# A spectral mixing layer feeding a snake MLP on one core: two groups of a batch's last transform stage go behind the next batch's first stage, and three idle matmuls are added in the head

## The chip, the core and the metric

The kernel runs on one core of a Trainium2 chip. The engines that matter here are PE (TensorE: matmuls, with its weight loads shown as PEld), ACT (ScalarE), DVE (VectorE), POOL (GpSimd) and SP (SyncE); the last two mostly issue DMAs in this kernel. Each engine works through its own list of instructions in the order in which the program wrote them, and engines wait for one another through semaphores. The metric is the device time of one execution in microseconds (us).

## The reference, cut to what matters

```python
batch, seq, dim = (8, 3008, 256)          # d_ff = 2048
X = np.fft.rfft(x, axis=1)
Y = X * (filt_r + 1j * filt_i)[None, :, :]
y = np.fft.irfft(Y, n=seq, axis=1)        # 24064 rows of 256
h = y.reshape(24064, 256) @ w_in
s = np.sin(alpha * h)
g = h + s * s / (alpha + 1e-09)
return g @ w_out                          # float32
```

Each of the 8 sequences is filtered in the frequency domain, and the filtered rows go through a two-layer network whose activation is the snake function.

## The kernel before, in words

**Transforms.** The length 3008 is split into 47 x 64. A batch goes through four matmul stages, with an elementwise product in the middle: `first` (a transform over 47 points, PSUM tiles `pa`), `forward` (over 64 points, `pb`), the product with the filter on DVE, `inverse` (`pc`) and `last` (`pd`), which writes the time-domain rows, transposed, into the SBUF array `y`. Between `first` and `forward`, and between `inverse` and `last`, the data goes through DRAM to change its layout: `first` stores to `d1` (SP queue) and `load_t2` loads from it (POOL queue). Batch 0 takes a path of its own in the head, with transposes on DVE in place of the trips through DRAM, and its last stage is `last_0(n0, n, ...)`: the group of `n` rows of the split that begins at `n0`, in two halves, `cb` 0 and `cb` 1. Each half is `n` small matmuls of 94 columns into one PSUM bank, and then a cast into `y`, on ACT for half 0 and on DVE for half 1. A group covers the columns 94 n0 to 94 (n0 + n) - 1 of `y`.

**The network.** `y` of a pair of batches is cut into chunks of 512 columns (one of the twelve of a pair is 384 wide). `hidden(k, jb)` computes one of 16 blocks of the hidden layer for chunk k: two matmuls (`ph`, one for each half `cb` of `y`), a sine on ACT (`cos_all`), and on DVE an operation that makes the activation `v`. `project(k, u)` multiplies `v` by `w2` (`po`, eight matmuls in a call), and now and then ACT copies the result out (`o`), which is stored by DMA.

**The order.** The order of instructions is written out by hand. The main loop runs in steps; a chunk takes 8 steps, k runs from 0. Step s (with j = s mod 8) issues `hidden(k, 2j)` and `hidden(k, 2j+1)`, then a slot at s, then the `project` calls of chunk k-1, then a slot at s + 0.5. So chunk 2, columns 1024 to 1535, begins at step 16, and it reads `y` columns that the groups at 11 (columns 1034 to 1409) and at 15 (1410 to 1785) write. Everything of the transforms is put into one list, `pending`, with a due step, and `slot` takes from its front what is due; a PE item that is less than a step late is taken alone:

```python
while pending and pending[0][0] <= at:
    if pending[0][2]:
        if run and pending[0][0] > at - 1:
            break
        run += 1
```

Batch 1's sixteen `first` matmuls are due at `6.9 + 0.35 * i`, so the last ones at 11.1, 11.45, 11.8 and 12.15; its `load_t2` are due at 12.5, and its first `forward` at 18. A `last_0` group that is called with `spread=True` doesn't issue its matmuls at once: it puts them into the list `between`, and `one_between()` takes one after each `hidden` matmul and after each second `project` matmul.

**Buffers.** PSUM has the pool `fps` (2 banks: `pa`, `pb`, `pc`, `pd`), `hps` (4 banks: `ph`, and in the head also the idle `warm` tiles and others) and `ops` (2 banks: `po`). A matmul that takes a bank over waits until the cast of the bank's previous tile is done.

**Who casts.** `evac` decides between ACT and DVE. Its counter moves on at every call, also where the caller names the engine:

```python
flip[0] = (flip[0] + 1) % 3
if flip[0] if on_act is None else on_act:
```

The `first` matmuls let the counter decide, the `last_0` groups name the engine; so moving a group among the `first` matmuls also changes which engine casts some of these.

**The head.** `warm_pe(n)` issues `n` matmuls on a tile of zeros, into an `hps` bank that nobody reads. After batch 0's first stage come `spread_alpha(0)` (12 matmuls, `al_bc`), `inverse_table(0)` and `inverse_table(1)` (32 transposes, `pse`, that read the table `d_t`, which a DMA brings), `spread_alpha(1)`, one idle matmul and the first `forward_0` blocks (`pb`). The lines: `warm_pe` 443, `spread_alpha` 354, `inverse_table` 432, `last_0` 409, `first` 206, `forward` 243, `hidden` 610 (matmul), 614 (sine) and 615 (DVE), `project` 630, casts 185 (ACT) and 187 (DVE), `load_t2` 235, the loop over the groups 709 and 710.

Of the kernel before, what the change touches and what calls it, by code (L numbers as in the profile page):

```python
# [71 lines left out]
def kernel(  # L72
# [276 lines left out]
    def spread_alpha(i):  # L349

        ps = hps.tile([128, 4, 128], FP32, name=f"al_bc_{i}", tag="h")
        for a in range(4):
            for k, part in enumerate(parts):
                nc.tensor.matmul(out=ps[:, a, :], lhsT=one[:, 4 * i + a:4 * i + a + 1].to_broadcast([128, 128]),
                                 rhs=part, start=(k == 0), stop=(k == 2))
        nc.scalar.copy(out=alpha[:, i // 2, 512 * (i % 2):512 * (i % 2) + 512], in_=ps.rearrange("p a b -> p (a b)"))
# [69 lines left out]
    def inverse_table(g):  # L426

        gs = slice(8 * g, 8 * g + 8)
        ps = ops.tile([128, 8, 128], FP16, name=f"pse_{g}", tag="o")
        for i in range(8):  # L430
            for a in range(2):
                nc.tensor.transpose(out=ps[64 * a:64 * a + 64, i, :],
                                    in_=d_t[:, 8 * g + i, 64 - 64 * a:128 - 64 * a], identity=id16)
        nc.scalar.mul(e1_0[:, gs, :], ps, -0.125)
# [3 lines left out]
    def warm_pe(n):  # L438

        warmed.append(n)  # L440
        ps = hps.tile([128, 512], FP32, name=f"warm_{len(warmed)}", tag="h")
        for i in range(n):
            nc.tensor.matmul(out=ps, lhsT=idle[:, 0:128], rhs=idle[:, 0:512], start=True, stop=True)
# [18 lines left out]
    for i in range(16):  # L462
# [7 lines left out]
        if i < 15 and i % 4 == 3:  # L470
            warm_pe((1, 2, 2, 1)[i // 4])
    spread_alpha(0)
    [inverse_table(g) for g in range(2)]
    spread_alpha(1)
    warm_pe((2, 2, 2, 1)[3])
# [205 lines left out]
    def put(at, fn, *args, pe=False):  # L681
        pending.append((at, len(pending), pe, fn, args))
# [23 lines left out]
    for jb in range(12, 16):  # L706
        put(5 + 0.5 * (jb - 12), weights_out, jb, 1)

    for n0, n, at in ((6, 5, 1.5), (11, 4, 11), (15, 4, 13), (19, 4, 14.4), (23, 4, 15.6), (27, 5, 16.8)):
        put(at, last_0, n0, n, fps, "f", True)  # L710
    for b in range(1, B):
        s = s1 if b == 1 else Spectral(b)
# [89 lines left out]
```

## Time and profile before

| | |
|---|---|
| runs | 773.33, 773.35 and 774.28 us; median 773.35 us |
| the profiled execution, its own time | 774.35 us |
| its span, first to last instruction | 772.6 us |
| granted PE clock | 1.00 |
| PE busy | 763.0 us, 99% of the span |
| DVE, ACT, POOL busy | 655.4, 610.9, 373.1 us |
| HBM traffic | 133 GB/s over the span |

The profile page gives, for one execution, the busy time of each engine, the chain of work that ended last, and the costliest groups of instructions. The timeline gives rows of the form: start in us, duration in us, engine, line of the kernel, operation, output<-inputs, shapes, number of instructions merged into the row, and, where the engine was idle before it, the idle time and what ended it. A matmul's duration runs from its start to the arrival of its last result, while the next matmul may start earlier. So a short stall of PE hides under the durations and is not shown as idle; it is read from the distance between starts. In the steady part of this kernel a `first` matmul (`pa`) takes 0.22 us from start to start, a `ph` of 512 columns 0.216, a `po` 0.109 and a `pd` 0.04.

### The profile page before, as it was taken

The numbers are of one execution on the slowest core, as the hardware profiler recorded it, in microseconds if no ns is written. First come the engines' busy times: TensorE is split into PE (matmuls) and PEld (weight loads), VectorE is DVE, ScalarE is ACT, GpSimd is POOL, SyncE is SP. The second block draws the span as 40 slices with busy tenths as digits, with TensorE's granted clock in tenths as the row PEclk, the third lists the DMA queues.
The fourth block names the chain that finished last, engine by engine and source line by source line (L and its number), as shares of the span: only waits on it lengthen the run. The fifth ranks groups of instructions, "written<-read, shape, count | busy, mean of one in ns | idle before, by whom it ended". The sixth has DMA issues, their size and how long they took to land.

```text
span 772.6 us, 17227 instructions
## 1 busy us (share of the span) xinstructions
PE 763.0 (99%) x6038; PEld 517.1 (67%) x6038; DVE 655.4 (85%) x1171; ACT 610.9 (79%) x1205; POOL 373.1 (48%) x652
## 2 busy tenths in 40 slices
PE   8999999999999999999999999999999999999997
PEld 4757766666666667666666676766666766766666
DVE  7887998999988888988889888899888888777774
ACT  6898987898787878877878787888778787777763
POOL 7555455644636456545555646644554645520000
PEclk9999999999999999999999999999999999999999
DMA  9945678854854437544574536754254322511112
GB/s 225 292 108 167 139 172 257 205 131 112 219 145 125 114 92 207 140 114 118 118 197 114 137 94 156 196 144 121 72 145 109 90 69 56 147 35 33 40 36 61
DMA packets 81598, 101.49 MB, mean 131 GB/s; under 512 B 18900, under 2 KB 60880, under 8 KB 81511
## 3 DMA queue, kind: packets, MB, share of 16 engines
q0 software_dynamic: 27520, 47.29, 26.0%
q1 hardware_dynamic: 53426, 52.41, 25.5%
q8 instruction: 47, 0.77, 0.4%
q10 hardware_dynamic: 565, 0.70, 0.3%
q14 instruction: 40, 0.33, 0.1%
HBM read 56.15 MB, written 46.66 MB: 133 GB/s over the span
## 4 chain that ended last, share of the span: by engine, by line
PE 89%; DVE 5%; DMA 2%; ACT 2%; POOL 1%; issue 1%; SPq 0%; POOLq 0%; DVEq 0%
PE po L630 40%; PE ph L610 40%; DVE v L615 3%; PE pd L316 2%; PE pb L243 2%; PE pa L222 2%; DMA xs<-xf 1%; PE pc L293 1%; DMA e_t<-e_tbl 1%; ACT cos_all L614 1%; DVE t_a L479 1%; ACT t_h L185 1%; PE pa L206 0%; PE pd L409 0%; POOL filt_t L365 0%
## 5 line engine op out<-in xcount | busy, mean ns | idle before, releaser
L615 DVE SCALAR_TENSOR_TENSOR v<-cos_all,ph 128x512 f16<-128x512 f32 (+1 forms) x768 | 482.5, 671 | 94.8 <-ACT cos_all L614 90.8
L614 ACT ACTIVATE cos_all<-ph 128x512 f32<-128x512 f32 (+1 forms) x768 | 414.1, 600 | 99.4 <-PE ph L610 98.8
L675 POOL DMA_DIRECT2D out_dram<-o x530 | 291.7, 557 | 246.0 <-ACT o L639 219.5
L610 PE MATMUL ph<-y,w 128*128 128x512 f16 (+1 forms) x1536 | 389.3, 375 | 1.6 <-DVE v L615 1.3
L630 PE MATMUL po<-w,v 128*128 128x256 f16 x3008 | 389.5, 273 | 0.0
L630 PEld LDWEIGHTS <-v 128*128 128x128 f16 x3008 | 290.0, 98 | 84.2 <-issue 0.9
L610 PEld LDWEIGHTS <-w 128*128 128x128 f16 x1536 | 143.3, 98 | 114.1 <-issue 19.3
L639 ACT COPY o<-po 128x512 f32<-128x512 f32 (+1 forms) x95 | 56.0, 590 | 7.7 <-PE po L630 6.8
L185 ACT CAST y<-pd 128x376 f16<-128x376 f32 (+1 forms) x86 | 42.0, 490 | 13.1 <-PE pd L316 8.8
L246 ACT CAST xf<-pb 128x512 f16<-128x512 f32 x84 | 51.0, 608 | 0.9 <-PE pb L243 0.2
L160 POOL DMA_DIRECT2D x<-in_x_dram x48 | 25.6, 538 | 39.0 <-DVE v L615 29.9
L185 ACT CAST t_h<-pa 128x512 f16<-128x512 f32 (+1 forms) x60 | 32.8, 589 | 12.6 <-PE pa L222 11.3
L316 PEld LDWEIGHTS <-t_a 96*128 96x128 f16 x448 | 31.4, 97 | 12.7
L264 DVE TENSOR_TENSOR p<-p,xs 128x512 f16<-128x512 f16 x84 | 35.7, 425 | 2.9
L263 DVE TENSOR_TENSOR xs<-xs,filt_t 128x512 f16<-128x512 f16 x84 | 35.1, 418 | 3.5 <-DMA xs<-xf 3.5
L257 DVE TENSOR_TENSOR p<-xf,filt_t 128x512 f16<-128x512 f16 x84 | 35.0, 418 | 0.0
L185 ACT CAST gt<-pc 128x512 f16<-128x512 f32 x54 | 28.1, 595 | 8.4 <-PE pc L293 8.4
L187 DVE CAST t_h<-pa 128x512 f16<-128x512 f32 (+1 forms) x52 | 33.5, 682 | 0.2
L243 PE MATMUL pb<-t,d_t 128*128 128x256 f16 x168 | 32.1, 273 | 0.0
L316 PE MATMUL pd<-wh_t,t_a 96*128 96x94 f16 x384 | 31.8, 204 | 0.0
L235 POOL DMA_DIRECT2D t<-d x28 | 24.4, 874 | 10.7 <-DMA d<-t_h 10.0
L243 PEld LDWEIGHTS <-d_t 128*128 128x128 f16 x168 | 16.4, 98 | 14.3
(72 smaller groups left out, 276.5 us busy)
## 6 DMA issues: line engine op xcount, KB each, us to landing
t<-d POOLq DMA_DIRECT2D x28, 384.0 KB, 5.0
xs<-xf SPq DMA_DIRECT2D x168, 64.0 KB
t_a<-d SPq DMA_DIRECT2D x28, 384.0 KB
x<-in_x_dram POOLq DMA_DIRECT2D x50, 188.0 KB, 4.4
d<-t_h SPq DMA_DIRECT2D x48, 192.0 KB
d<-gt SPq DMA_DIRECT2D x36, 256.0 KB
out_dram<-o POOLq DMA_DIRECT2D x91, 64.0 KB, 2.1
out_dram<-o POOLq DMA_DIRECT2D x31, 80.0 KB, 3.3
```

The lines of the kernel that those rows point to most:

```text
L185: marks["act"] = nc.scalar.copy(out=dst, in_=src)
L243: nc.tensor.matmul(out=ps[:, i, :], lhsT=d_t[:, s, :], rhs=self.t2[s // 6][:, s % 6, :], start=True, stop=True)
L246: nc.scalar.copy(out=self.xf[u], in_=ps)
L263: nc.vector.tensor_tensor(out=xs, in0=xs, in1=f_t[1][:, 2 * u:2 * u + 2, :], op=ALU.mult)
L264: nc.vector.tensor_tensor(out=p, in0=p, in1=xs, op=ALU.add)
L316: nc.tensor.matmul(out=psv[:, i, :], rhs=wi_t if self.b < TILED else wh_t, start=True, stop=True, lhsT=t4_h[ch // 2][0:NK, n0 % 16 + i, cb ...
L610: nc.tensor.matmul(out=ps[:, 0:n], lhsT=w1[:, cb, jb * 128:jb * 128 + 128], rhs=y_cols[:, cb, c0:c0 + n], start=(cb == 0), stop=(cb == 1))
L614: nc.scalar.activation(out=cs[:, 0:n], in_=ps[:, 0:n], func=AFT.Sin, bias=float(np.pi / 2))
L615: marks["snake"] = nc.vector.scalar_tensor_tensor(out=v[k][:, jb, 0:n], in0=cs[:, 0:n], scalar=-1.0, in1=ps[:, 0:n], op0=ALU.add, op1=ALU. ...
L630: nc.tensor.matmul(out=pso[k][:, t % 2, :], lhsT=v[k][:, jb, 128 * t:128 * t + 128], rhs=w2[:, jb, :], start=(jb == 0), stop=(jb == 15))
L639: copy(out=o[:, i0:t % 2 + 1, :], in_=pso[k][:, i0:t % 2 + 1, :])
L675: queues[i % len(queues)].dma_start(out=bass.AP(tensor=out.tensor, offset=out.offset + t0 * C, ap=[*ap, [1, C]]), in_=o_blk[p0:p0 + rows, :])
```

## The change

```diff
@@ -470,6 +470,7 @@
         if i < 15 and i % 4 == 3:
             warm_pe((1, 2, 2, 1)[i // 4])
     spread_alpha(0)
+    warm_pe(3)
     [inverse_table(g) for g in range(2)]
     spread_alpha(1)
     warm_pe((2, 2, 2, 1)[3])
@@ -706,7 +707,7 @@
     for jb in range(12, 16):
         put(5 + 0.5 * (jb - 12), weights_out, jb, 1)
 
-    for n0, n, at in ((6, 5, 1.5), (11, 4, 11), (15, 4, 13), (19, 4, 14.4), (23, 4, 15.6), (27, 5, 16.8)):
+    for n0, n, at in ((6, 5, 1.5), (11, 4, 12.2), (15, 4, 13.2), (19, 4, 14.4), (23, 4, 15.6), (27, 5, 16.8)):
         put(at, last_0, n0, n, fps, "f", True)
     for b in range(1, B):
         s = s1 if b == 1 else Spectral(b)
```

Three idle matmuls of 512 columns go between `spread_alpha(0)` and the transposes of `inverse_table`, into one `hps` bank. The group at 11 goes from due step 11 to 12.2, behind batch 1's `first` matmuls 12 to 15; the group at 15 goes from 13 to 13.2. No other due step changes, and nothing else is added or removed.

## The prediction

> **What bounds the kernel.** I read the page's first part and the chain, then the busy time in stretches, then the timelines of the two places that the change touches.
>
> ```profile
> PE 763.0 (99%) x6038; PEld 517.1 (67%) x6038; DVE 655.4 (85%) x1171; ACT 610.9 (79%) x1205; POOL 373.1 (48%) x652
> PE 89%; DVE 5%; DMA 2%; ACT 2%; POOL 1%; issue 1%; SPq 0%; POOLq 0%; DVEq 0%
> ```
>
> PE is the bound and carries 89% of the chain. The stretches (start:end, length, then busy PE, PEld, DVE, ACT, POOL, clock, DMA) say whether a delay of PE can be made up later:
>
> ```profile
> 55.00:64.00 9.00, 8.79 (x71) 6.76 (x70) 5.52 (x10) 7.92 (x17) 3.67 (x7) 1.00 0.44 130
> 64.00:70.00 6.00, 6.00 (x58) 5.02 (x56) 4.45 (x9) 4.77 (x10) 5.48 (x9) 1.00 0.57 164
> 70.00:109.00 39.00, 39.00 (x285) 27.59 (x283) 37.22 (x76) 34.39 (x68) 21.75 (x42) 1.00 0.71 161
> ```
>
> From 70 to 109 us PE is busy 39.00 of 39.00, and start to start it runs at its pace there. There is no idle time to give a delay back: what PE has lost when `forward` begins (69.46) it keeps to the end. So the sum is the difference of PE's waits up to there.
>
> **The three idle matmuls.** PE in the head:
>
> ```profile
> 12.08 0.83 PE L354 MATMUL al_bc<-w,one 128*128 128x128 bf16 x12
> 13.62 1.08 PE L432 MATMUL pse<-w,d_t 128*64 128x128 f16 x32 [0.70 <-DMA d_t<-d_tbl]
> 14.64 0.84 PE L354 MATMUL al_bc<-w,one 128*128 128x128 bf16 x12
> 15.32 0.38 PE L443 MATMUL warm<-idle 128*128 128x512 f16 x1
> 15.53 1.49 PE L497 MATMUL pb<-t_a,d_t 128*128 128x128 f16 x12
> ```
>
> Twelve `al_bc` at 0.056 start to start leave PE free at 12.75; the transposes start at 13.62, when the table `d_t` has landed. Three idle matmuls at 0.217 (15.32 to 15.53) take 0.65 and end their turn at 13.40. Their bank was last cast by DVE, from `pa` 12 of batch 0, done by 12.03. So they cost 0, and the cover is the landing of `d_t`. If it lands earlier, up to 0.65 is exposed at the transposes, but not behind them: `pb` at 15.53 needs DVE's second transpose, whose row (12.96, 2.37 long) ends at 15.33, so at most some 0.15 gets through. Below zero: at most what a clock drop would have cost, and there is none in the rows (a rival, below). They also shift the four-bank rotation by one: the second `al_bc` now waits for ACT's cast of `pa` 13 (done by 12.2), the first `pb` for ACT's copy of `al_bc` (12.96 to 13.54). All lie before their use at 14.6 and 15.5: 0. I take 0, ends -0.05 and +0.15.
>
> **The moved groups, before.** I call batch 1's `first` matmuls pa 0 to 15 and the halves of the groups 11a, 11b, 15a and so on. PE, in rows from there:
>
> ```profile
> 55.39 0.38 PE L206 MATMUL pa<-x,wf_t 94*96 94x512 f16 x1
> ...
> 56.61 0.20 PE L409 MATMUL pd<-wi_t,t_a 128*128 128x94 f16 x1
> 56.81 0.38 PE L206 MATMUL pa<-x,wf_t 94*96 94x512 f16 x1
> 57.37 0.38 PE L206 MATMUL pa<-x,wf_t 94*96 94x512 f16 x1 [0.19 <-ACT y L185]
> ...
> 63.26 0.38 PE L630 MATMUL po<-w,v 128*128 128x256 f16 x2
> 63.61 0.20 PE L409 MATMUL pd<-wi_t,t_a 128*128 128x94 f16 x1
> ...
> 64.42 1.03 PE L610 MATMUL ph<-y,w 128*128 128x512 f16 x4
> ```
>
> These are pa 11, the end of 11a, pa 12, pa 13, the start of 19b and chunk 2. By starts, pa 12 waits 0.16 (56.65 to 56.81, for the cast of pa 11), pa 13 0.34 (57.03 to 57.37, for the cast of 11a), 11b 0.06, pa 15 0.18, 19b 0.13 and the first `forward` 0.03: **0.90 us**. The reader is to see that only 0.19 of it is shown as idle. Chunk 2 waits for nothing: 15b was cast at 63.01 (below), 1.4 us ahead of it.
>
> **The moved groups, after.** The matmuls are the same; the order changes, and with it the casts. In the new program's order pa 12 and pa 15 are cast by DVE (0.68 each) instead of ACT (0.58); 13 and 14 stay on ACT. Rows for the prices, ACT first, DVE second:
>
> ```profile
> 56.18 0.58 ACT L185 CAST t_h<-pa 96x512 f16<-96x512 f32 x1
> ...
> 62.91 0.61 ACT L614 ACTIVATE cos_all<-ph 128x512 f32<-128x512 f32 x1 [0.53 <-PE ph L610]
> 63.46 0.48 ACT L185 CAST y<-pd 128x376 f16<-128x376 f32 x1
> 63.83 0.62 ACT L614 ACTIVATE cos_all<-ph 128x512 f32<-128x512 f32 x1
> ```
>
> ```profile
> 62.41 0.69 DVE L615 SCALAR_TENSOR_TENSOR v<-cos_all,ph 128x512 f16<-128x512 f32 x1 [0.24 <-ACT cos_all L614]
> 63.01 0.54 DVE L187 CAST y<-pd 128x376 f16<-128x376 f32 x1
> 63.54 0.69 DVE L615 SCALAR_TENSOR_TENSOR v<-cos_all,ph 128x512 f16<-128x512 f32 x1
> ```
>
> ACT spaces its instructions 0.5 after a sine and 0.37 after a 376-column cast, DVE 0.60 after `v`; an engine starts some 0.04 after what it waits for has ended.
>
> *Gain.* pa 11 at 55.39, eight `po` (0.87), pa 12 at 56.48 without a wait, since no group has taken a bank between. pa 13 could start at 56.70 and waits for the cast of pa 11 (56.18 + 0.58 + 0.05 = 56.81): 0.11. pa 14 and 15 find their banks free. Of the 0.90, the first four terms (0.74) become 0.11.
>
> *Loss.* Everything of group 15 now lies directly ahead of chunk 2. On from pa 13: two hidden blocks, pa 14 at 57.9, eight `po`, pa 15 at 59.0; then 11a, 11b, 15a and 15b, each 1.03 with the blocks or `po` it is woven into: hidden block 14 at 61.29, 15b's first matmul due at 62.54 and started at 62.65 (its bank holds 11b, which DVE casts behind two `v`: 0.11), chunk 2's first matmul at 63.47. That one reads half 0, cast long ago; the second, at 63.73 behind one `pd`, reads half 1 and needs 15b's cast. On its path: block 14's second matmul starts at 61.55 and ends at 61.93; ACT's sine of block 14 at 61.97, the cast of 15a at 62.52 (its last matmul ends at 62.49), the sine of block 15 at 62.90, ended at 63.50; DVE's `v` of block 15 at 63.53, and behind it the cast of 15b at 64.13, ended at 64.67. The matmul starts at 64.72: a wait of **0.99 us** that the kernel before doesn't have. Behind it stand chunk 2's other matmuls, 19a and the `po`; PE works in order, so all of them wait.
>
> *Smaller ones.* Groups 19, 23 and 27 follow a slot later than before. 23b waits 0.11 for its bank (as 19b did), the first `forward` 0.22 for DVE's cast of 23b, 27b 0.37 for ACT's cast of 27a, which stands behind the first cast of `forward`. After: 0.11 + 0.11 + 0.99 + 0.11 + 0.22 + 0.37 = **1.91 us**. Difference 1.91 - 0.90 = **+1.0 us**. Its ends: 0.99 goes to 0 if the cast is in time (+0.0, and -0.9 with no wait at all), and to 2.2 if DVE's two new casts of 0.60 both stand in its path (+2.2).
>
> *Queues.* Two DMAs depend on the moved casts: the last store of `first` on SP and the four `load_t2` on POOL, whose row shows a wait of 5.79 for that store (64.52). The cast of pa 15 moves from 60.36 to 59.57 and ends 0.7 earlier; store and loads come 0.7 earlier. As `forward` showed no DMA wait at 69.46, this is worth 0. Other DMAs keep their order in both queues.
>
> **Sum.** 0 + 1.0. The profiled execution took 774.35 (a span of 772.6 and 1.75 around it), 1.0 over the median of the runs, 773.35. Against its own time the new kernel comes to 775.4 with a span of 773.6; against the median to **774.4 us**, +0.13%.
>
> **Rivals.**
> 1. *The wait at chunk 2 isn't there or is covered:* the gain of 0.63 stands against the smaller waits alone, 773.4; without these, 772.7. For it: DVE has idle rows (0.24 ahead of 62.41). Against: DVE can't run the `v` of block 15 before ACT's sine, and the sine not before PE. Chance 0.13.
> 2. *Slower, on the other side of the bound:* DVE comes to block 14 late, because it took over two casts of 0.60. One of them in the path of 15b's cast makes the wait 1.6 and the time 775.0, both 775.6. It decides from 0.5 us more than I count. Against: I find both casts done before DVE's `v` of block 12 (60.5). Chance 0.20.
> 3. *The idle matmuls are not hidden:* 0.65 more, 775.0, if neither DVE's transposes nor the wait of 0.24 for `e_t` at 19.91 take it up. Chance 0.03.
> 4. *The gap in the head costs a slow clock in the usual execution, and the idle matmuls mend it.* The kernel's first twelve idle matmuls took 0.43 each, against 0.217 later: PE can be at half pace. Were it so from 13.62 to 15.53, that would cost 1.9, and its mending gives 772.5. Against: the clock is 1.00 in the page there, and the pairs of transposes behind the gap follow at 0.056, the pace of `al_bc` ahead of it. Chance 0.02. The Trainium skill ("TensorE: Matmul & The Clock Gate", Part 1: The HAM clock gate) says that PE falls to half its clock after an idle window of about 3.4 us. By that rule a gap of 0.70 is too short, and the trace agrees.
>
> **How the numbers follow.** A measurement of this kernel tells about 0.2% (1.55 us) from no change: the runs before differ by 0.95. The bounds are 771.8 and 774.9. My forecast has 0.57; it lies 0.5 from the upper bound, and I give 0.05 more to its slipping over through the spread of runs. Something that I don't see and that gains over 1.55: 0.05. Slower: 0.05 + 0.20 + 0.03 = 0.28; faster 0.05; within: 0.52 + 0.13 + 0.02 = 0.67. The range reaches to 773.2 (rival 1's upper case, leaving out about 0.14 below) and to 775.6 (rival 2, about 0.06 above).
>
> **What would show it.** Right: the transposes still start at about 13.6, with the idle matmuls at 12.75 to 13.4 and a shorter idle in front; PE waits about 0.8 to 1.0 by starts at chunk 2's second `ph`, put down to DVE's cast of `y`; pa 13 in place by 56.8; `pb` of `forward` some 0.5 later and the next chunk's blocks 1.0 later than before. Wrong: no wait at that `ph`, or one over 1.5; transposes past 13.7; or a new PE wait after 75 us.

## The result and the profile after

| | before | after |
|---|---|---|
| median of 21 runs each | 773.72 us | 775.83 us |
| ratio after / before, 95% interval | | 1.0032 [1.0019, 1.0044] |
| the profiled execution, its own time | 774.35 us | 775.14 us |
| its span | 772.6 us | 773.4 us |

The changed kernel is slower by 0.32%: 2.1 us by the medians, 2.5 us by the ratio, with 1.5 to 3.4 in the interval. The prediction said 774.4 with a range to 775.6, so the time lies 0.2 us above the range. Of the 1.4 us between 774.4 and 775.83, 0.37 is the base: the three runs that the prediction started from had a median of 773.35, the 21 runs 773.72. The other 1.1 us is cost that the sum didn't have. In five of the 21 runs of the changed kernel the granted clock was 0.996 to 0.998 and the time 777.0 to 782.0 us; the median of the other sixteen is 775.66.

The profiled execution shows only 0.8 us of it, 773.4 against 772.6. It falls into three parts, taken from the starts of the `ph` matmuls: the head is 0.6 shorter in this execution (the table `d_t` landed at 13.35 instead of 13.57, and `e_t`, which the first `inverse` matmuls of batch 0 read, at 19.04 instead of 19.86), the middle, from the first `ph` to chunk 3's first, is 1.08 longer, and the rest, nearly all of it in one spot near 528 us, gives 0.3. A single pair of executions therefore can't be subtracted; the stretches have to be.

The page of the changed kernel, its busy time by engine:

```profile
PE 763.1 (99%) x6041; PEld 516.9 (67%) x6041; DVE 656.9 (85%) x1173; ACT 609.8 (79%) x1203; POOL 373.3 (48%) x652
```

The three idle matmuls are the three more on PE (6041), and two casts have gone from ACT to DVE (1203 and 1173 against 1205 and 1171). PE is the bound as before. The idle matmuls took one more line of the program, so line 610 of the kernel before is 611 here, and so on.

The head, PE's timeline of the changed kernel:

```profile
12.48 0.81 PE L443 MATMUL warm<-idle 128*128 128x512 f16 x3
13.39 1.08 PE L432 MATMUL pse<-w,d_t 128*64 128x128 f16 x32
```

The idle matmuls start at 12.48 and end their turn at 12.48 + 3 x 0.217 = 13.13. The transposes (`pse`) start at 13.39, 0.04 after `d_t` landed. In this execution the idle matmuls delayed nothing.

The place where chunk 2 begins, PE first, then DVE and ACT:

```profile
62.88 0.38 PE L611 MATMUL ph<-y,w 128*128 128x512 f16 x1
63.09 0.20 PE L409 MATMUL pd<-wi_t,t_a 128*128 128x94 f16 x1
64.12 0.38 PE L611 MATMUL ph<-y,w 128*128 128x512 f16 x1 [0.83 <-DVE y L187]
```

```profile
62.92 0.69 DVE L616 SCALAR_TENSOR_TENSOR v<-cos_all,ph 128x512 f16<-128x512 f32 x1 [0.24 <-ACT cos_all L615]
63.52 0.54 DVE L187 CAST y<-pd 128x376 f16<-128x376 f32 x1
```

```profile
61.91 0.47 ACT L185 CAST y<-pd 128x376 f16<-128x376 f32 x1
62.28 0.61 ACT L615 ACTIVATE cos_all<-ph 128x512 f32<-128x512 f32 x1
```

Chunk 2's first matmul starts at 62.88; the second could follow one `pd` later, at 63.13, and starts at 64.12: a wait of 0.99. It ends 0.06 after DVE's cast of 15b (63.52 + 0.54), and the cast stands behind the `v` of block 15, which stands behind ACT's sine of 62.28, which stands behind the cast of 15a: the chain of the prediction link by link, everything 0.6 earlier because the head was.

The stretches of the changed kernel (start:end, length, then busy PE, PEld, DVE, ACT, POOL, clock, DMA):

```profile
55.00:64.00 9.00, 8.30 (x67) 6.45 (x66) 7.36 (x12) 6.86 (x14) 3.89 (x8) 1.00 0.42 119
64.00:70.00 6.00, 5.83 (x53) 5.02 (x53) 4.27 (x8) 4.28 (x9) 5.74 (x10) 1.00 0.85 245
70.00:109.00 39.00, 38.78 (x285) 27.56 (x283) 36.77 (x76) 34.21 (x67) 20.30 (x41) 1.00 0.65 145
```

PE, which was busy 8.79, 6.00 and 39.00 there, now has 0.70, 0.17 and 0.22 idle, and nothing after it gets that back: behind chunk 2 the distances between `ph` matmuls are those of before, apart from a few spots that are told below. The list of PE's waits has two new entries of this stretch, the second for 27b:

```profile
PE ph L611 <- DVE y L187: 0.8, 1, 0.8
...
PE pd L409 <- ACT xf L246: 0.2, 1, 0.2
```

### The profile page after: what moved, and what is told of

It reads as the page before. It is cut to its first block, busy times and chain, and to the rows that moved or that the text cites. A ratio compares the mean times of both kernels' runs of the same rounds, so it can differ in the third digit from the quotient of the medians.

```text
span 773.4 us, 17230 instructions
## 1 busy us (share of the span) xinstructions
PE 763.1 (99%) x6041; PEld 516.9 (67%) x6041; DVE 656.9 (85%) x1173; ACT 609.8 (79%) x1203; POOL 373.3 (48%) x652
## 4 chain that ended last, share of the span: by engine, by line
PE 88%; DVE 5%; DMA 3%; ACT 2%; issue 1%; POOL 1%; SPq 0%; ACTq 0%; DVEq 0%; POOLq 0%
PE po L631 39%; PE ph L611 39%; DVE v L616 4%; PE pd L316 2%; PE pb L243 2%; DMA xs<-xf 2%; PE pa L222 1%; DMA d_t<-d_tbl 1%; ACT cos_all L615 1%; PE pc L293 1%; PE pc L521 1%; PE pb L498 1%; PE warm L443 1%; PE pa L206 0%; PE pc L274 0%
## 5 line engine op out<-in xcount | busy, mean ns | idle before, releaser
L257 DVE TENSOR_TENSOR p<-xf,filt_t 128x512 f16<-128x512 f16 x84 | 35.1, 419 | 0.0
```

## The experiments

The question was where the 1.1 us come from that the sum didn't have. Every time below is the median of 10 to 12 runs, and its ratio goes against 27 to 35 runs of the kernel before on the same chip, whose median is named with each group; 0.1% is 0.77 us. "Middle" is the time from the first `ph` to chunk 3's first, which holds all of the moved groups' effect: 45.34 us in the profile of before, and 45.35 in two more traces of the same program. The first two groups of runs were made on one chip, the next two on a second chip, the last on a third.

### The two parts alone, both, and the wait shortened (before 773.65)

Only the idle matmuls:

```diff
     spread_alpha(0)
+    warm_pe(3)
     [inverse_table(g) for g in range(2)]
```

> The kernel before with the three idle matmuls alone. The change measured +2.1 us by medians, while the profiled executions differ by 0.8, of which the groups' waits give +1.05 and the head -0.6. Theory A (the groups, and through their long PE wait the clock: it drops in some executions): 773.4 to 774.0, as before. Theory B (the idle matmuls are exposed in the head in most executions, as in rival 3): +0.6 to +1.1, 774.3 to 774.8. Theory C (the excess is the spread of executions): as before, 773.4 to 774.4.

Measured: 774.56 us, ratio 1.0011 [0.9994, 1.0027].

Only the groups:

```diff
-    for n0, n, at in (..., (11, 4, 11), (15, 4, 13), ...):
+    for n0, n, at in (..., (11, 4, 12.2), (15, 4, 13.2), ...):
```

> The changed kernel without the three idle matmuls: the two groups moved alone. Theory A: the whole +2.1 us, with granted clocks of 0.996 to 0.999 in a third to half of the executions. Theory B: +1.05 us (the sum of the waits: 1.95 against 0.9 by starts), clocks 1.00. Theory C: +1.05 us and clocks as in the kernel before. In the trace all have the wait of 0.99 at chunk 2's second matmul.

Measured: 775.44 us, ratio 1.0018 [1.0009, 1.0026]. The middle is 1.05 longer, and the same wait stands at chunk 2.

The whole change, with 15b cast by ACT instead of DVE, so that it doesn't stand behind the `v` of block 15:

```diff
-                    evac(y[:, cb, 0, n0:n0 + n, :], made[0], cb == 0)
+                    evac(y[:, cb, 0, n0:n0 + n, :], made[0], cb == 0 or n0 == 15)
```

> The changed kernel with one edit: the second half of the group at 15 is cast by ACT, right behind the sine of block 15, instead of by DVE behind the v of block 15. That shortens the path of the long wait by about 0.5: the cast ends near 64.2 on the clock of the earlier timeline, so PE waits 0.45 to 0.5 in place of 0.99. All theories expect -0.5 us against the changed kernel in the profile. Theory A expects more in the median than that, some -1.0 to -1.5, because the shorter wait no longer lets the clock drop; theories B and C expect -0.5.

Measured: 775.24 us, ratio 1.0017 [1.0006, 1.0028]. PE and ACT in its timeline:

```profile
63.17 0.38 PE L611 MATMUL ph<-y,w 128*128 128x512 f16 x1
63.90 0.38 PE L611 MATMUL ph<-y,w 128*128 128x512 f16 x1 [0.30 <-ACT y L185]
```

```profile
63.37 0.47 ACT L185 CAST y<-pd 128x376 f16<-128x376 f32 x1 [0.18 <-PE pd L409]
```

The wait is 63.90 - 63.17 - 0.25 = 0.48 instead of 0.99; PE is now released by ACT, and the middle is 0.54 shorter than with the cast on DVE. So the wait at chunk 2 is DVE's cast and its place in DVE's list, and its length can be set from there. The runs are too few to show the gain in the time: it is 0.2 below the whole change by the medians, 0.5 by the ratios, with intervals that overlap.

The whole change again:

> The changed kernel itself, on the same chip and beside the same runs of the kernel before as the three others, as their measure. If its excess of 2.1 us over the kernel before is a property of the kernel (A, B), it comes out at +1.8 to +2.4 again; by C it comes out anywhere from +1.0 to +2.1.

Measured: 775.44 us, ratio 1.0023 [1.0012, 1.0033]. Together the four say that the result repeats, that the granted clock has no part in the cost of the groups (0.999 or more in every run of the groups alone), that the groups make most of the result, and that the idle matmuls may cost something. Groups 1.4 and idle matmuls 0.85 by these ratios add up to 2.25, within the 1.8 to 2.5 of the whole. But the medians of the groups alone and of the whole change are the same, 775.44: on top of the groups the idle matmuls show 0.4 by the ratios, which is not told from 0.

### Is the comparison itself off, and what do more idle matmuls do? (before 774.17)

The kernel before in the place of a changed one:

> The kernel before, unchanged, measured in the place of a changed kernel. All four kernels so far came out 0.7 to 1.0 us above what their traces account for in the part that was changed, with or without the moved groups, with or without the idle matmuls, and with clocks at 0.999 or more in nearly all executions; theory A (the clock drops) has fallen by that. Theory N (the excess belongs to the comparison: the runs of the kernel before that it is compared with sit lower than any kernel in this place): this one comes out at 774.3 to 774.6 too, +0.7 to +0.9. Theory K (the edits themselves cost something that the profiled executions don't show): 773.4 to 773.8, within 0.2 us of the runs of the kernel before.

Measured: 774.02 us, ratio 0.9995 [0.9985, 1.0004]. No excess of the comparison itself is seen; a second time, against 773.77, it gave 773.79 and 0.9996 [0.998, 1.0013] (the third group).

Nine idle matmuls instead of three, in the kernel before:

> The kernel before with nine idle matmuls in front of the transposes in place of the three. They take 1.95 us against the 0.87 of the gap, so the transposes start at about 14.7 instead of 13.6, or as late as the table lands if that is later. If the cover in the head is what the prediction took it for (DVE's transposes until 15.33, then the wait for e_t at 19.91), part of the 1.1 is taken up by the 0.4 of that wait: +0.6 to +0.9 us at the first hidden block against an execution whose table lands at the same time. If the head is bound by something else behind the transposes, less than 0.3 arrives there. In the median: theory N adds 0.7 to 0.9 to that, theory K nothing.

Measured: 775.39 us, ratio 1.0014 [1.0004, 1.0024]. Its head:

```profile
12.78 2.10 PE L443 MATMUL warm<-idle 128*128 128x512 f16 x9
14.81 1.08 PE L432 MATMUL pse<-w,d_t 128*64 128x128 f16 x32
```

`d_t` had landed at 13.72, so here PE, and not the DMA, sets the start: the transposes come at 14.81, 1.19 later than in the profile of before, and 0.78 of that is left where the first `ph` starts (35.63 against 34.84). This is what idle matmuls look like when they are not hidden, and no trace with three of them looks so.

The group at 11 at step 9 instead, ahead of more of the `first` matmuls:

```diff
-    ..., (11, 4, 11), ...
+    ..., (11, 4, 9), ...
```

> The kernel before with the group at 11 moved the other way, from step 11 to step 9. By the same reckoning as in the prediction PE's waits from the first batch's groups on come to 0.7 in place of 1.0 us, so the stretch from hidden block 56.4 to chunk 3 is 0.27 us shorter in the trace. In the median: -0.3 by theory K, +0.4 to +0.6 by theory N. It is the best order of the groups that I found, and it would be the version to keep if it is not slower.

Measured: 773.7 us, ratio 0.9992 [0.9982, 1.0002]; the middle is 0.24 shorter. A new wait has come in place of others: PE is idle for 0.42 ahead of the `first` matmul at 45.95, until ACT's cast of an earlier one is done. It is the best of the variants, and not told from no change.

### A plain pause, and the two parts again (before 773.77)

Five matmuls without use, directly ahead of chunk 2 in the kernel before, about as long as what the groups add:

```diff
+    def pause():
+        ps = hps.tile([128, 512], FP32, name="pause", tag="h")
+        for i in range(5):
+            nc.tensor.matmul(out=ps, lhsT=w1[:, 0, 0:128], rhs=w1[:, 0, 0:512], start=True, stop=True)
+    put(15.5, pause)
```

> The kernel before, its groups in their old places, with a pause of PE of the same size at the same place: five idle matmuls (1.08 us) directly ahead of chunk 2. By the reckoning from the rows the blocks behind it come 1.09 later in the trace and nothing else changes. Theory P (a delay of PE there has a price of its own beyond its length, since it shifts all later transfers against each other): the median is +1.7 to +2.1 over the kernel before, as with the moved groups. Theory G (only the moved groups have the excess of some 0.7, through the other casts or the earlier loads): +1.0 to +1.2. Theory S (the excess is between the sets of runs, which have differed by 0.5 in the kernel before alone): +1.0 to +1.2 here, and the repeat of the moved groups below falls to +1.0 to +1.4.

Measured: 775.78 us, ratio 1.0022 [1.0003, 1.004]. The middle is 1.08 longer, as the five matmuls make it. The interval reaches from 0.2 to 3.1 us, so whether 1.08 us of lost PE time costs 1.08 at the end or more is not told by it (1.7 by the ratio, 2.0 by the medians); at least it isn't given back.

The kernel before again (the result stands above), and the groups alone and the idle matmuls alone again:

> The kernel before, unchanged, as the measure of how far two sets of runs of one kernel lie apart on one chip. All theories: within 0.4 us of the runs of the kernel before. What it tells is the size of that distance (0.15 the first time).

> The moved groups alone, a second time. Theory G and P: +1.6 to +2.0 over the kernel before and over its twin in this set. Theory S: +1.0 to +1.4.

Measured: 774.99 us, ratio 1.0018 [1.0009, 1.0026], as the first time by the ratio, though by the medians the excess is 1.2 after 1.8. The middle is 1.07 longer.

> The three idle matmuls alone, a second time; the first gave +0.9 with an interval from -0.5 to +2.1. In the profiled execution they filled the gap and nothing behind it came later. Theory S, and the prediction: -0.3 to +0.3 over the kernel before and its twin. If they do cost something that the profiled executions don't show, +0.6 to +1.0 again.

Measured: 774.99 us, ratio 1.0011 [1.0002, 1.0019], as the first time. Weighed together, the two measurements of the idle matmuls alone give 0.11% with about 0.03 to 0.19%, so 0.85 us with 0.3 to 1.4. And yet the trace of this run shows them hidden as well. Two of PE's waits in its head:

```profile
PE pc L521 <- DMA e_t<-e_tbl: 0.8, 1, 0.8
PE pse L432 <- DMA d_t<-d_tbl: 0.4, 1, 0.4
```

PE still waits 0.4 for `d_t` with the three idle matmuls done, and once more, 0.8, for `e_t` behind it.

### Where the idle matmuls stand, and how many (before 773.77)

Three matmuls of the same size at the program's end, behind the last projection; one instead of three in the gap; three ahead of the first `spread_alpha`:

> The kernel before with three idle matmuls behind the last projection, where PE has nothing left to do while the last copies and stores run (PE's last start is at 768.1 of 772.6). In the trace they cost nothing. Theory K2 (a program that differs from the kernel before by a few instructions measures some 0.9 higher, wherever they stand, since the head's transfers land at other times): +0.6 to +1.0 over the kernel before. Theory H (the idle matmuls cost their 0.9 in the head): 0, within 0.4.

> One idle matmul (0.22 us) in the gap in place of three (0.65). Theory H with a cost that goes by PE's time: a third of 0.9, +0.2 to +0.4. Theory H with a cost of the break itself, or theory K2: +0.6 to +1.0. In the traces so far the transposes started 0.04 after the landing of their table in every execution, with the idle matmuls and without, so the prediction's own step says 0.

> Three idle matmuls one place earlier, ahead of the first twelve matmuls that spread alpha, so that the same 0.65 us of PE are used, but the gap in front of the transposes is left as a gap of some 0.2. The transposes wait for the table as before. If it is the amount of idle work in the head (theory H), +0.6 to +1.0 as with the three behind. If it is the program (K2), the same. If it is the place directly in front of the transposes, 0, within 0.4.

| | time | ratio |
|---|---|---|
| three at the end | 773.74 us | 1.0003 [0.9992, 1.0014] |
| one in the gap | 774.18 us | 1.0001 [0.9991, 1.0012] |
| three ahead of `spread_alpha` | 774.18 us | 1.0009 [0.9999, 1.0020] |

Three more instructions of the kind at the end show no cost, but with -0.6 to 1.1 us in the interval this doesn't exclude 0.85. In the head there is a tendency by the ratios: one 0.1, three 0.7 to 0.85, nine 1.1 us. The intervals of neighbours overlap, and by the medians one in the gap and three ahead of `spread_alpha` are alike.

### The jam of transfers near 330 us (before 773.94)

One place far behind the change comes and goes between executions of the same kernel. DVE's waits from 325 to 348 us, in the profile of before, in another execution of the same program, and in the changed kernel, in this order:

```profile
DVE xs L263 <- DMA xs<-xf: 1.9, 1, 1.9
```

```profile
DVE xs L263 <- DMA xs<-xf: 0.4, 1, 0.4
```

```profile
DVE xs L263 <- DMA xs<-xf: 1.8, 1, 1.8
```

`xs`, a copy of a `forward` result with its halves exchanged, is loaded on SP's queue while an `x` load, two stores of `d` and a `t` load are under way. In the sixteen traces with this order of loads, DVE waits 1.5 to 2.1 for it in seven, and PE loses 0.5 to 1.1 us between 337 and 348 us in just these (0.85 in the profile of before); it waits 0.4 to 1.0 in nine, and PE loses nothing. With three idle matmuls in the gap, four of five traces have this loss (1.07, 0.78, 0.58, 1.03); of the eleven others three have it (0.85, 0.95, 0.49). The means are 0.69 and 0.21, a difference of 0.5 us. The first expectation below says eight of sixteen traces and four of the eleven; by DVE's waits it is seven and three. So the theory was that the idle matmuls shift the program against its transfers so that they jam here more often. To take the jam away, the last quarter of the `x` load is issued four steps earlier for batches 4 to 7:

```diff
-                put(22 + 4 * ch if b == 2 else firsts(b)[ch] - 8, s.load_x, ch)
+                put(22 + 4 * ch if b == 2 else firsts(b)[ch] - (12 if b > 3 and ch == 3 else 8), s.load_x, ch)
```

This was run by itself, with the idle matmuls, with the whole change, and with the group at step 9:

> The kernel before with one load moved: the last quarter of x of the batches 4 to 7 is fetched 12 steps ahead of its first stage instead of 8. Where the traces of one kernel differ behind the head, it is most often at one place, near 340 us: there PE loses 0.5 to 1.07 us in 8 of 16 profiled executions and nothing in the others, and DVE waits up to 2.1 us for xs<-xf, whose transfer was issued at 330, among the load of x (328.7), two stores of d and a load of t, which fill the queues. Theory Q (the excess of the idle matmuls is that this jam occurs more often with them: it is there in 4 of 5 traces with the three in the gap, in 4 of 11 others): without the jam the median is 0.2 to 0.5 us under the kernel before, with no loss at 340 in the trace. Theory H (a cost in the head): the same for this kernel, and the next one tells.

> The same with the three idle matmuls in the gap. Theory Q: within 0.3 us of the one without them. Theory H: +0.6 to +1.0 over it, as the idle matmuls measured over the kernel before.

> The same with the whole change. Theory Q: +1.05 us over the first of these kernels, the waits of the groups alone. Theory H: +1.7 to +2.1. In the trace the stretch from hidden block 32 of chunk 1 to chunk 3 is longer by 1.05, as in all the others.

> The earlier load together with the group at 11 moved to step 9, the version that came out lowest so far (771.1 in its profile). By the waits it is 0.23 under the first of these kernels; 773.0 to 773.5 in the median, 0.4 to 0.8 under the kernel before.

| with the earlier load | time | ratio | DVE's wait for `xs` near 330 | middle, against before |
|---|---|---|---|---|
| alone | 773.92 us | 1.0002 [0.9994, 1.0011] | none | -0.01 |
| + three idle matmuls | 773.61 us | 0.9997 [0.9988, 1.0006] | none | -0.01 |
| + the whole change | 774.97 us | 1.0017 [1.0008, 1.0026] | none | +1.05 |
| + group at step 9 | 773.77 us | 1.0004 [0.9989, 1.0019] | none | 0.00 |

The edit does what it was made for: in all four traces the wait for `xs` has gone and PE loses nothing there. In this setting the idle matmuls show no cost (773.61 against 773.92), and the whole change costs 774.97 - 773.92 = 1.05 us by the medians, as much as the middle shows. But this group ran on another chip than those that showed the 0.85, and the idle matmuls were not run there without the earlier load; so it is not shown whether the load or the chip makes the difference. Two expectations failed. The earlier load alone was to gain by taking the jam out of the kernel before, and it doesn't. With three jams in eleven traces that gain would be 0.2 us, which the interval (-0.5 to +0.8) can't tell from none. And with the group at step 9 the time was to be 773.0 to 773.5; it is 773.77, and the gain of 0.24 in the middle is not there either: the wait ahead of that `first` matmul was 0.69 in this execution instead of 0.42.

## Why the prediction was right or wrong

**The moved groups: right, in mechanism and size.** By starts, the changed kernel's waits against the prediction's:

| wait of PE | predicted | measured |
|---|---|---|
| pa 13, for the cast of pa 11 | 0.11 | 0.11 |
| 15b, for its bank | 0.11 | 0.13 |
| chunk 2's second `ph`, for the cast of 15b | 0.99 | 0.99 |
| 23b, for its bank | 0.11 | 0.14 |
| first `forward`, for the cast of 23b | 0.22 | 0.21 |
| 27b, for the cast of 27a | 0.37 | 0.38 |

Their difference to the waits of before was put at 1.0, and every trace with the moved groups, alone or with the idle matmuls, has a middle that is 1.05 to 1.08 longer. The signs that the prediction named are there: no wait in front of pa 12, the wait at chunk 2 put down to DVE's cast of `y`, `pb` 0.5 later and chunk 3's start 1.08 later once the head's 0.6 is taken off. That the delay is carried to the end one to one holds, too: no stretch behind it is shorter for it. By the runs the groups cost 1.4 us twice, with 0.7 to 2.0 in the interval; 1.05 lies inside, so nothing shows more than the waits.

**The queues at 0: no sign against it.** `forward` waits for DVE's cast in the changed kernel, and not for `load_t2`, whose first load landed 2.4 us ahead of it. In the kernel before that cover was thinner than a wait of zero suggests: it was 1.0 us in the profile (landed at 68.47, `forward` at 69.46), and in the trace with nine idle matmuls, where no group is moved, `forward` does wait for that load, and the middle is 0.66 longer for it.

```profile
PE pb L243 <- DMA t<-d: 0.5, 1, 0.5
```

This is the list of PE's waits of that kernel from 60 to 85 us; the wait is its only entry.

**The rivals.** No wait at chunk 2: refuted by the 0.99. DVE late by its two new casts: the `v` of block 15 starts 0.03 after its sine, so DVE was not late. Idle matmuls exposed at the transposes: refuted in that form, since the transposes start 0.04 after `d_t` lands with and without them, in every trace but that with nine. A slow clock that they mend: the kernel with them alone is not faster, and the transposes behind the gap run at their pace in both.

**The idle matmuls at 0: as far as the runs tell, this is the step that failed.** The prediction costed them at 0, with ends of -0.05 and +0.15, since the landing of `d_t` covers them. They are covered, as every trace with three of them shows, and yet the two measurements of them alone come to 0.85 us (0.3 to 1.4) together. By that they are the larger part of the 1.1 us that the sum lacked, and the 0.4 between 1.4 and 1.05 for the groups is the rest, which may be chance. The size is less sure than its interval says: on top of the groups the idle matmuls show 0.4, and with the earlier load, on another chip, nothing. The flaw in the reasoning is that it followed a single execution's chain at the place of the change, and took what is hidden there as free everywhere. It also followed the shift of the bank rotation, which any number of idle matmuls in the gap causes, in the head alone; but one idle matmul shifts it as three do and showed 0.1 (-0.7 to 0.9).

**The base.** The sum started from the median of three runs, which was 0.37 below that of 21. From 773.72 the same range would have reached 775.97 and held the time, but by luck: its upper part stood for a late DVE, which the trace doesn't show.

**What stays open** is where the 0.85 lies. It is not the clock, which was 0.999 or more in all but one run of each of the two measurements; not the comparison, as far as two tries of the kernel before against itself tell; and not a delay of the transposes in any trace with three of them. The head shows no more either: the first `ph` comes 14.9 to 15.1 us after the first `pc`, the matmul that needs `e_t`, in all traces, and it starts at 34.8 on the mean of the seven traces with three idle matmuls in the gap and at 35.1 on that of the twelve with fewer, between 34.2 and 37.3. A candidate is the jam near 330 us: the loss is more frequent in traces with the idle matmuls (4 of 5 against 3 of 11, a split that chance alone gives about once in 13, at a place that was picked after seeing the traces), it is worth 0.5 us on the mean by these counts, and with the jam taken away no cost of the idle matmuls is seen. Against: that was on another chip, taking the jam away from the kernel before gained nothing, the means leave 0.35 unexplained, the measurement with the earlier load (-0.9 to +0.5 against before) overlaps a little with 0.3 to 1.4, and no run shows how 0.65 us of work that ends before its cover does could reach transfers 300 us later. So the jam is not shown to be the cause. The idle matmuls alone with the old load, run on the third chip beside those with the earlier load, would tell the load from the chip.

## What to carry to other kernels

When a group of work is moved, list every cast that follows it and ask which engine casts it and what that engine has in front: the stall here was read to 0.01 us from the order of three lists and the duration of four kinds of instruction, and putting one cast on the other engine halved it. Work hidden beside a transfer is free on the chain that one trace shows; here the runs put 0.3 to 1.4 us on it for a reason that was not found, so give it a price above zero, and take the range wider than the local bounds and the base from more than three runs. To read effects of 0.1%, compare stretches between fixed landmarks in several traces and 20 or more runs: two single spans differ by more than that.

## What the runs showed of the hardware

- The same loads in the head land at different times from execution to execution: `d_t` at 13.3 to 14.9 us and `e_t` at 19.0 to 22.3 us over the traces, and the first `ph` follows, from 34.2 to 37.3. This scatter goes into the span, and in a pair of traces it can be larger than the whole effect of the change.
- PE's pitch for 512 columns falls from 0.43 to 0.216 us at a time that differs between executions, 4.2 to 7.5 us after the start, 2.7 to 6.0 after the first matmul. The Trainium skill ("TensorE: Matmul & The Clock Gate", Part 1: The HAM clock gate) says that the window by which the clock is released runs freely, so that the number of slow matmuls varies between runs. The traces agree that it varies; the section names a variation of 0.5 us either way, and the 2.7 to 6.0 here are wider. No cost is seen here: with the release at 7.45 and at 4.72 the first `ph` starts at 34.84 and 34.80.
- An execution can lose 0.5 to 1.1 us of PE time in one spot (near 330 us) when a wait for one transfer is 1.5 to 2.1 us long instead of 0.4 to 1.0; the same program had 1.9 in one execution and 0.4 in another. Smaller losses of 0.2 to 0.8 us appear near 112, 141 and 528 us in some traces. With one load issued four steps earlier, the first of them was gone in all of four traces, and the time of the kernel before with it was the same (773.92 against 773.94 us).
